# A place of its own for one summed weight block, and other steps for its transfers, for a weight split and for earlier sums

## The chip, the cores and the metric

The kernel runs on one core of a Trainium2 chip. The metric is the time of one execution on the device in microseconds (us); for several runs it is their median.

## The reference, cut to what matters

```python
xn = layernorm(x)                       # x: 1 x 2048 x 576
q, k, v = split(xn @ wqkv)              # 32 heads of 18
pq, pk = phi(q), phi(k)                 # phi(t) = (t + 1 if t > 0 else exp(t)) + 1e-6
o = (pq @ (pk^T v)) / (pq . sum(pk) + 1e-6)   # per head
s = o @ wo
h = gelu(xn @ w1 + b1)                  # 576 -> 4608
g = silu(h @ w2 + b2)                   # 4608 -> 576
out = x + s * g
```

All arrays are float32.

## The kernel before, in words

Each float32 operand of a product is split into a rounded part (hi, a cast on ScalarE) and what is left (lo, a subtraction, mostly on VectorE); three products of such parts stand for one. Large products go by a Strassen-like scheme with seven block products instead of eight. The blocks that it needs besides the plain ones are sums or differences of blocks, made ahead.

The kernel has two parts. The first (up to about 290 us) makes the normalised x, the keys and values and their state, then, in rounds `r` of 14 steps, the queries and the attention output. The second is the feed-forward network. It works in two halves of 1024 rows; each half has nine chunks (`NC`) of 512 of the 4608 hidden columns. A chunk has two `Up` products (x times w1, seven block products each, then gelu), followed by seven block products with w2, numbered in the order 1, 2, 7, 4, 5, 3, 6, each in two parts (`product`, line 1279 for the matmul). A product of a pair 2 after 1, 4 after 7, 3 after 5 goes on in the bank of the earlier one, after VectorE has added that one's result to `macc` (lines 1287 and 1289).

The order is written by hand. A chunk has 28 steps (`NS`): 0 to 13 are the block products of the two Ups, 14 to 27 the halves of the seven products. `add(base + k, f, ...)` puts a call at step k, and `at_step` makes the calls of a step, in the order in which they were added, after that step's matmuls have been issued. TensorE, VectorE, ScalarE and GpSimd (POOL) keep the written order in this part; each engine works through its own instructions one after another, and an instruction that must wait holds up those behind it. SyncE (SP) issues the plain transfers, in its own order.

What the chunk's steps do, as far as the change and its neighbours go:

- `HOps.S(i, pr)`: POOL makes the sums of h for the pair `pr` (lines 1237 to 1246), i = 7, 5, 6, 3; for pair 0 at steps 7, 8, 10, 11, for pair 1 at 13, 14, 15, 15. `hi` (line 912) and `lo` (line 915) split them.
- `W1.T(i)`: POOL makes the differences of w1's blocks (lines 937 to 945), i = 5, 6, 7, 4; 7 and 4 overwrite the loaded block. A chunk does this twice: at steps 0 to 2 for its own second Up (table `P1`), and at steps 24 and 25 for the next chunk's first (table `P0`). Difference 4 overwrites a part of what the block "a" is split from.
- `W2`: the w2 operands of the next chunk. `load_raw` loads four blocks into one buffer (`w2raw`), which the chunk's own operands 1, 7 and 3 still read at steps 3, 4 and 6. Operand 7 is block (0, 1) plus block (1, 1), operand 4 is block (0, 0) plus (1, 0) plus operand 7. These sums are made by transfers that POOL issues and that add to what they find in place (`add_to`, line 497). Before the change, operand 7 is summed in `w2raw` itself, operand 4 in a tile of its own, `w2t4`, that is loaded right after the raw blocks.
- In the rounds of the queries, `w2_load` loads raw w2 blocks, `w2_sum` makes sums in the same accumulating way, and `w2_hi` and `w2_lo` split and store them (lines 506 and 511) for use in the second half and the first chunk.

Steps of the changed transfers in a chunk, before: raw load at 8 (10 in chunk 0); the sum of operand 7 and the first of operand 4, one right after the other, at 16 (17); operand 2's split and then operand 4's second sum at 21 (22); operand 4's split at 27.

Of the kernel before, what the change touches and what calls it, by code (L numbers as in the profile page):

```python
# [8 lines left out]
F32 = mybir.dt.float32  # L9
# [6 lines left out]
P = 128  # L16
S = 2048
D = 576
HD = 288
# [7 lines left out]
CF = 4  # L27
NC = NF // CF
# [14 lines left out]
def linear_attention_gated_ffn(ctx, tc, x, wqkv, wo, w1, b1, w2, b2, out):  # L43
    nc = tc.nc
# [96 lines left out]
    class Weight:  # L141

        def __init__(self, pool, name):
            self.h, self.l = (pool.tile([P, 7, 2, HD], F32R, name=f"{name}_{v}") for v in "hl")
            self.rh, self.rl = (pool.tile([P, D], F32R, name=f"{name}_r{v}") for v in "hl")
# [328 lines left out]
    def w2_blocks(c):  # L474
        return w2[c].rearrange("p (r n a d) -> p r n a d", r=2, n=2, a=2)
# [41 lines left out]
    def add(step, fn, *args):  # L517
        plans.setdefault(step, []).append((fn, args))
# [195 lines left out]
    for p in range(1, NPAIR):  # L714
        plan_pair(p)
        base = p * NSP
# [23 lines left out]
    def q_tiles(r):  # L740
        return [r_bufs[(2 * r + s) % 4] for s in range(2)]
# [11 lines left out]
    base = NPAIR * NSP  # L753
# [237 lines left out]
    for r in range(NPAIR + 2):  # L991
        base = (NPAIR + r) * NSP
# [3 lines left out]
        if r < NPAIR:  # L996
            a, b = q_tiles(r)
# [15 lines left out]
        if 1 <= r < NPAIR:  # L1013
            a, b = q_tiles(r)
# [10 lines left out]
        if 2 <= r <= 6:  # L1025
            add(base, w2_load, r + 2, *((w1p, "wa") if r % 2 == 0 else (w2rp, "w2raw")))
        if r == 2:
            add(base + 8, w2_sum, 2 * r + 5)
        if 3 <= r <= 7:
            n = 2 * r + 3  # L1030
            add(base + 1, w2_sum, n + 1)
            if r < 7:
                add(base + 8, w2_sum, n + 2)
            for j in range(2):
                add(base + 7 + j, w2_hi, n + j)
                add(base + 9 + j, w2_lo, n + j)
        if r == 0:
            phi_exp(a, e_bufs[0]), phi_exp(b, e_bufs[1])
            fold_wo({
# [74 lines left out]
    fr = ctx.enter_context(tc.tile_pool(name="fr", bufs=1, side="right", reuse_waits="tile"))  # L1114
# [67 lines left out]
    class W2:  # L1182


        def __init__(self, n):
            self.n, self.ops, self.tiles = n, {}, {}

        def load_raw(self):
            self.raw = raw = load_w2_raw(self.n) if self.n else w2_raw0[0]
            self.B = lambda r, n: raw[:, r, n]  # L1190
            self.src = {1: self.B(0, 0), 2: self.B(1, 0), 3: self.B(1, 1), 7: self.B(0, 1)}
            if 0 < self.n < NC:
                self.src[4] = fr.tile([P, CF // 2, HD], F32, tag="w2t4", name=f"w2t4_{self.n}", bufs=1)
                nc.sync.dma_start(self.src[4], w2_blocks(self.n)[:, 0, 0])

        def sum7(self):
            add_to(self.src[7], w2_blocks(self.n)[:, 1, 1])
# [235 lines left out]
    def plan_w1(add, w, base, T, hi, lo):  # L1433
        for table, what in ((T, w.T), (hi, w.hi), (lo, w.lo)):
            for i, at in table.items():
                add(base + at, what, i)
# [3 lines left out]
        hi={"a": 0, 6: 1, 7: 2, 5: 3, "b": 4, 4: 4},  # L1440
        lo={"a": 0, 6: 1, 7: 2, 5: 3, "b": 4, 4: 4},
    )
    P0 = dict(
        T={5: 24, 6: 24, 7: 25, 4: 25},
        hi={"a": 14, 6: 25, 7: 26, 5: 26, "b": 27, 4: 27},
        lo={"a": 14, 6: 25, 7: 26, 5: 26, "b": 27, 4: 27},
    )


# [7 lines left out]
        hi={  # L1457
            (1, 0): 7, (2, 0): 9, (7, 0): 10, (1, 1): 11, (2, 1): 12, (7, 1): 15, (4, 0): 16,
            (4, 1): 17, (5, 1): 18, (5, 0): 19, (6, 0): 20, (3, 0): 21, (3, 1): 22, (6, 1): 23,
        },  # L1460
        lo={
            (1, 0): 9, (2, 0): 10, (7, 0): 11, (1, 1): 12, (2, 1): 13, (7, 1): 15, (4, 0): 16,
            (4, 1): 17, (5, 1): 18, (5, 0): 19, (6, 0): 20, (3, 0): 21, (3, 1): 22, (6, 1): 23,
        },
# [4 lines left out]
    w2t = {}  # L1469
# [5 lines left out]
    for step in range(n_chunks):  # L1475
        half, c = divmod(step, NC)
        base = step * NS
        plain = step == n_chunks - 1
        h = HOps(c)
        if half == 0:  # L1480
            plan_w1(add, w1t[2 * step + 1], base, **P1)
            w2c = w2t[step]
            if not step:
                add(base + 2, w2c.sum7)
            for i, at in (PW2 if step else PW2_FIRST).items():
                add(base + at, w2c.hi, i)
                add(base + at, w2c.lo, i)
            if step == 0:
                for i, at in W2_SUMS_FIRST.items():
                    add(at, w2t[0].load, i)  # L1490
        if half == 0 and c < NC - 1:
            add(base + 0, make, W1, w1t, 2 * step + 2)
            add(base + 4, make, W1, w1t, 2 * step + 3)
            add(base + 13, lambda n=2 * step + 2: plan_w1(add, w1t[n], base, **P0))
            make(W2, w2t, step + 1)
            nxt = w2t[step + 1]
            add(base + (8 if step else 10), nxt.load_raw)
            add(base + (16 if step else 17), nxt.sum7)
            add(base + (16 if step else 17), nxt.sum4, 0)
            add(base + 21, nxt.hi, 2)  # L1500
            add(base + 21, nxt.lo, 2)
            add(base + (21 if step else 22), nxt.sum4, 1)
            add(base + 27, nxt.hi, 4)
            add(base + 27, nxt.lo, 4)
            for i, at in W2_SUMS_NEXT.items():
                add(base + at, lambda i=i, n=step + 1: w2t[n].load(i))
        elif not plain:
            add(base + (14 if half == 0 else 7), make, W1Loaded, w1t, 2 * step + 2)
            swap = half == 0
            add(base + (22 if swap else 14), make, W1Loaded, w1t, 2 * step + 3)  # L1510
            if step + 2 < n_chunks:
                make(W2, w2t, step + 1)
                for i, at in W2_NEXT.items():
                    add(base + at + 11 * swap, lambda i=i, n=step + 1: w2t[n].load(i))
            else:
                make(W2, w2t, step + 1)
                add(base + 7, w2t[step + 1].load_raw)
        if not plain:
            if half == 0 and c == NC - 1:
                for k, at in ((2, 12), (3, 12), (1, 13), (0, 13)):  # L1520
                    add(base + at, x_swap, k)
                add(base + 25, silu_first, C11)
                for k in range(2):
                    add(base + 26 + k, combine, C12, nc.vector, slice(2 * k, 2 * k + 2))
                    add(base + 26 + k, combine, C21, nc.gpsimd, slice(2 * k, 2 * k + 2))
            for what in ("S", "hi", "lo"):
                for (i, pr), at in PH[what].items():
                    add(base + at, getattr(h, what), i, pr)
        else:
            for f in range(CF):  # L1530
                w2t[step].plain(f)
                add(base + (1, 2, 3, 8)[f], w2t[step].hi, ("p", f))
                add(base + (2, 3, 8, 9)[f], w2t[step].lo, ("p", f))
        if half == 1 and c == 0:
            add(base, silu_first, C12)
            add(base, silu_first, C21)
            add(base, combine, C22, nc.vector, slice(0, 2))
            add(base + 1, combine, C22, nc.vector, slice(2, 4))
            add(base + 1, silu_first, C22)
        if half == 1 and 1 <= c <= 8:  # L1540
            for k in range(2):
                tiles = {}
                def load(k=k, t=7 + c, tiles=tiles):
                    tiles[0] = finish_tiles(k)
                    finish_load(t, k, tiles[0])
                add(base, load)
                add(base + 4, lambda k=k, t=7 + c, tiles=tiles: finish(t, k, tiles[0]))
        if plain:
            for m in (C12, C21, C22):
                add(base + 4, combine, m, nc.gpsimd)  # L1550
            for t, at in enumerate((5, 5, 7, 13, 5, 12, 12, 12)):
                add(base + at, load_xs, t)
            for b, f, at, lo in (
                (0, 0, 7, 8), (0, 1, 8, 9), (1, 0, 10, 10), (1, 1, 10, 11), (0, 2, 11, 12),
                (0, 3, 12, 13), (1, 3, 13, 13), (1, 2, 13, 13),
            ):
                add(base + at, tail_split, b, f)
                add(base + lo, tail_lo, b, f)
        for j in range(CF // 2):
            n = 2 * step + j  # L1560
            u = Up(n, w1t.pop(n), xs)
            for k, i in enumerate(UP):
                u.step(i)
                h.add(j, u.g)
                at_step(base + 7 * j + k)
        if plain:
            break
        held = {}
        for k, i in enumerate(ORDER):
            for q2 in (0, 2):  # L1570
                product(c, i, q2, [h.ops[i, 0], h.ops[i, 1]], w2t[step].ops[i], held)
                at_step(base + 14 + 2 * k + q2 // 2)
# [36 lines left out]
```

## Time and profile before

| | |
|---|---|
| median of 3 runs | 1119.4 us (1118.47 to 1122.9) |
| the profiled execution | 1122.14 us |
| its span, first to last instruction | 1120.4 us |
| TensorE busy | 1098.9 us, 98% |
| VectorE busy | 810.8 us, 72% |
| ScalarE busy | 505.4 us, 45% |
| POOL busy | 459.5 us, 41% |
| TensorE's mean granted clock | 0.996 |
| moved by DMA | 272.50 MB, mean 243 GB/s |

In the profile's rows an instruction is named by its engine, line and operation, then `output<-inputs` by the program's tile names, and partitions x elements of each. PE is TensorE's matmul, PEld its weight load, DVE VectorE, ACT ScalarE, and SPq a transfer issued by SP. In a row in order of time the first number is the start and the second the duration, in us; the square brackets hold the idle time of the engine before it and what ended that. In a row of a stretch, the first number is its length, then come busy time and (x) number of instructions for PE, PEld, DVE, ACT and POOL, then the granted clock, the busy share of the 16 DMA engines and GB/s.

### The profile page before, as it was taken

What the parts mean: (1) busy time and instruction counts of PE and PEld (TensorE: products, weight loads), DVE (VectorE), ACT (ScalarE), POOL (GpSimd) and SP (SyncE); (2) the same over time, 40 slices, a digit from 0 to 9 for tenths busy, and PEclk for the clock granted to TensorE, in tenths of its full rate; (3) what the DMA queues carried; (4) which work ended last, traced back from release to release, by engine and by line L of the source; (5) the groups of instructions that cost most, each with busy time, mean ns of one, the idle gap of its engine ahead of it and who ended that gap; (6) DMA issues with size and microseconds to landing.
All of it is one profiled execution on the core that took longest, in us unless ns stands there. A gap on an engine that the chain in (4) does not pass through costs nothing.

```text
span 1120.4 us, 18755 instructions
## 1 busy us (share of the span) xinstructions
PE 1098.9 (98%) x6924; PEld 1017.2 (91%) x6924; DVE 810.8 (72%) x1242; ACT 505.4 (45%) x913; POOL 459.5 (41%) x419
## 2 busy tenths in 40 slices
PE   8999999999999999999999999999999999999997
PEld 7899998999898998988989889899898998988987
DVE  6877666656598888988889888666475574664756
ACT  6766554535545454454544544524233242242352
POOL 5854433344354444544545434324224132242340
PEclk9999999999999999999999999999999999999999
DMA  5887747895998679687796879977666666766243
GB/s 202 299 265 275 257 129 216 275 293 197 349 313 336 198 267 316 190 333 225 246 320 180 318 208 373 369 263 261 216 200 225 206 203 210 230 198 223 87 135 120
DMA packets 95818, 272.50 MB, mean 243 GB/s; under 512 B 10413, under 2 KB 21165, under 8 KB 93679
## 3 DMA queue, kind: packets, MB, share of 16 engines
q1 hardware_dynamic: 89391, 258.32, 65.2%
q0 software_dynamic: 6336, 12.98, 7.4%
q8 instruction: 55, 0.90, 0.3%
q14 instruction: 36, 0.29, 0.1%
HBM read 165.05 MB, written 100.01 MB: 237 GB/s over the span
## 4 chain that ended last, share of the span: by engine, by line
PE 90%; DVE 4%; ACT 3%; DMA 1%; issue 1%; POOL 1%; DVEq 0%; POOLq 0%; ACTq 0%
PE pm L1279 32%; PE e L1141 12%; PE a L1141 10%; PE zy L1141 10%; PE ps_s L885 5%; PE pl L411 5%; PE b L1141 4%; PE e L356 2%; PE z L356 2%; PE a L356 2%; PE pd L1402 2%; DVE h_l L915 1%; PE ps_kva L464 1%; DMA kr<-kw 1%; PE b L356 1%
## 5 line engine op out<-in xcount | busy, mean ns | idle before, releaser
L912 ACT CAST h_h<-g 128x512 fp32r<-128x512 f32 x204 | 120.1, 621 | 140.6 <-PE pm L1279 139.5
L915 DVE TENSOR_TENSOR h_l<-g,h_h 128x512 fp32r<-128x512 f32 x204 | 169.3, 830 | 0.0
L1287 DVE TENSOR_TENSOR macc<-macc,pm 128x576 f32<-128x576 f32 x128 | 96.1, 751 | 36.8 <-PE pm L1279 36.7
L1246 POOL TENSOR_TENSOR mid<-g 128x512 f32<-128x512 f32 x34 | 44.0, 1294 | 184.7 <-ACT g L1149 184.7
L1141 PE MATMUL a<-xH,wa 128*128 128x512 f32 x360 | 117.1, 390 | 0.0
L1289 DVE TENSOR_TENSOR macc<-pm,macc 128x576 f32<-128x576 f32 x90 | 68.0, 755 | 18.4 <-PE pm L1279 17.6
L1149 ACT ACTIVATE g<-b,b1c 128x512 f32<-128x512 f32 x36 | 24.8, 688 | 124.5 <-DVE b L1167 124.5
L1141 PEld LDWEIGHTS a<-xH,wa 128*128 128x128 f32 x360 | 67.6, 188 | 13.7
L1141 PE MATMUL e<-xSH,wb 128*128 128x512 f32 x216 | 66.6, 390 | 0.2 <-DVE b L1167 0.2
L1240 POOL TENSOR_TENSOR g<-g 128x512 f32<-128x512 f32 x34 | 49.5, 1456 | 22.3 <-DVE h_l L915 20.9
L1158 ACT COPY mid<-a 128x512 f32<-128x512 f32 x36 | 21.2, 588 | 83.0 <-PE a L1141 82.6
L1141 PE MATMUL a<-xL,wa 128*128 128x512 f32 x144 | 56.2, 391 | 0.0
L1373 POOL TENSOR_TENSOR fin1l<-fin1h,fin1l 128x288 f32<-128x288 f32 x8 | 6.4, 806 | 120.0 <-DMA fin1l<-s_dram 61.6
L1243 POOL TENSOR_TENSOR g<-g 128x512 f32<-128x512 f32 x34 | 49.9, 1467 | 13.1 <-DVE h_l L915 11.8
L1237 POOL TENSOR_TENSOR g<-g 128x512 f32<-128x512 f32 x34 | 50.9, 1496 | 2.7
L1161 DVE TENSOR_TENSOR mid<-b,mid 128x512 f32<-128x512 f32 x36 | 24.7, 685 | 37.5 <-PE b L1141 37.4
L1141 PE MATMUL b<-xSH,w 128*128 128x512 f32 x144 | 50.2, 389 | 0.0
L1141 PE MATMUL zy<-xSH,w 128*128 128x512 f32 x144 | 50.2, 389 | 0.0
L1141 PE MATMUL e<-xSH,w 128*128 128x512 f32 x144 | 50.2, 389 | 0.0
L1141 PE MATMUL zy<-xH,w 128*128 128x512 f32 x144 | 50.2, 389 | 0.0
L1141 PEld LDWEIGHTS e<-xSH,wb 128*128 128x128 f32 x216 | 40.5, 188 | 9.1 <-DVE b L1167 0.6
L915 DVE TENSOR_TENSOR h_l<-mid,h_h 128x512 fp32r<-128x512 f32 x34 | 42.4, 1248 | 6.6 <-ACT h_h L912 6.6
(930 smaller groups left out, 3570.1 us busy)
## 6 DMA issues: line engine op xcount, KB each, us to landing
op<-w SPq DMA_DIRECT2D x72, 256.0 KB
w<-op SPq DMA_DIRECT2D x72, 256.0 KB
w1raw<-w SPq DMA_DIRECT2D x18, 640.0 KB
w2raw<-w SPq DMA_DIRECT2D x10, 1152.0 KB
op_a<-wa SPq DMA_DIRECT2D x18, 640.0 KB
wa<-op_a SPq DMA_DIRECT2D x18, 640.0 KB
op<-w2o SPq DMA_DIRECT2D x19, 576.0 KB
w2r<-w SPq DMA_DIRECT2D x6, 1152.0 KB
```

The lines of the kernel that those rows point to most:

```text
L356: nc.tensor.matmul(ps, st, mv, start=first and n == 0, stop=n == len(seq) - 1, skip_group_check=True,)
L411: nc.tensor.matmul(self.ps[n], st, self.wk(hl, k, n), start=(i == 0), stop=(i == n_all - 1))
L885: nc.tensor.matmul(self.ps[h], st[:, k, :], w[:, k, h * HD : (h + 1) * HD], start=(i == 0), stop=(i == len(self.seq) - 1),)
L912: nc.scalar.copy(pair[0], src)
L915: eng.tensor_tensor(pair[1], src, pair[0].bitcast(F32), op=SUB)
L1141: nc.tensor.matmul(ps.rearrange("p (c j) -> p c j", c=4), st, mv, start=first and n == 0, stop=n == len(seq) - 1, skip_group_check=True,)
L1237: tt(src[5, pr], A(1, 1), A(1, 0), op=SUB)
L1240: tt(src[6, pr], src[5, pr], A(0, 0), op=ADD)
L1243: tt(src[3, pr], src[6, pr], A(0, 1), op=SUB)
L1279: nc.tensor.matmul(ps[:, q, :HD], hs[p][st][:, cs], m[:, p, :], start=(n == 0 and i not in CHAIN), stop=(n == len(seq) - 1), skip_group_ch ...
L1287: nc.vector.tensor_tensor(dst, dst, src, op=SUB)
L1289: nc.vector.tensor_tensor(dst, src, dst, op=ADD)
```

## The change

In the first half's chunks operand 7 gets a tile of its own, `w2t6`, and operand 4 takes `w2t5` instead of `w2t4` (both names are used again only at the very end). Each tile is loaded by a call of its own, `load_sum`: operand 4's at step 0 with its first sum at step 4, operand 7's at step 6 with its sum at step 12. Operand 4's second sum, which adds operand 7, moves to step 20. The raw load stays at its step, and its block (0, 1) is no longer read from chunk 1 on. In table `P0` the split of w1's block "a" (cast, subtraction and store) moves from step 14 to step 24. In the queries' rounds the sum of a chunk's first block moves from step 8 to 5 of the round, and the split of the second block by one step (the cast from 8 to 9, the subtraction and store from 10 to 11).

```diff
         if r == 2:
-            add(base + 8, w2_sum, 2 * r + 5)
+            add(base + 5, w2_sum, 2 * r + 5)
         if 3 <= r <= 7:
             n = 2 * r + 3
             add(base + 1, w2_sum, n + 1)
             if r < 7:
-                add(base + 8, w2_sum, n + 2)
+                add(base + 5, w2_sum, n + 2)
             for j in range(2):
-                add(base + 7 + j, w2_hi, n + j)
-                add(base + 9 + j, w2_lo, n + j)
+                add(base + (7, 9)[j], w2_hi, n + j)
+                add(base + (9, 11)[j], w2_lo, n + j)
...
         def load_raw(self):
             self.raw = raw = load_w2_raw(self.n) if self.n else w2_raw0[0]
             self.B = lambda r, n: raw[:, r, n]
-            self.src = {1: self.B(0, 0), 2: self.B(1, 0), 3: self.B(1, 1), 7: self.B(0, 1)}
-            if 0 < self.n < NC:
-                self.src[4] = fr.tile([P, CF // 2, HD], F32, tag="w2t4", name=f"w2t4_{self.n}", bufs=1)
-                nc.sync.dma_start(self.src[4], w2_blocks(self.n)[:, 0, 0])
+            self.src |= {1: self.B(0, 0), 2: self.B(1, 0), 3: self.B(1, 1)}
+
+        def load_sum(self, i):
+            n = self.n
+            self.src[i] = fr.tile([P, 2, HD], F32, tag=f"w2t{5 + i // 7}", name=f"w2s{i}_{n}", bufs=1)
+            nc.sync.dma_start(self.src[i], w2_blocks(n)[:, 0, i // 7])
...
     P0 = dict(
         T={5: 24, 6: 24, 7: 25, 4: 25},
-        hi={"a": 14, 6: 25, 7: 26, 5: 26, "b": 27, 4: 27},
-        lo={"a": 14, 6: 25, 7: 26, 5: 26, "b": 27, 4: 27},
+        hi={"a": 24, 6: 25, 7: 26, 5: 26, "b": 27, 4: 27},
+        lo={"a": 24, 6: 25, 7: 26, 5: 26, "b": 27, 4: 27},
     )
...
             if not step:
+                w2c.src[7] = w2c.B(0, 1)
                 add(base + 2, w2c.sum7)
...
             nxt = w2t[step + 1]
+            add(base + 0, nxt.load_sum, 4)
+            add(base + 4, nxt.sum4, 0)
+            add(base + 6, nxt.load_sum, 7)
+            add(base + 12, nxt.sum7)
             add(base + (8 if step else 10), nxt.load_raw)
-            add(base + (16 if step else 17), nxt.sum7)
-            add(base + (16 if step else 17), nxt.sum4, 0)
             add(base + 21, nxt.hi, 2)
             add(base + 21, nxt.lo, 2)
-            add(base + (21 if step else 22), nxt.sum4, 1)
+            add(base + 20, nxt.sum4, 1)
             add(base + 27, nxt.hi, 4)
             add(base + 27, nxt.lo, 4)
```

More of the change, by code (lines that the diff above doesn't have):

```diff
@@ L1185, in __init__ @@
         def __init__(self, n):
-            self.n, self.ops, self.tiles = n, {}, {}
+            self.n, self.ops, self.tiles, self.src = n, {}, {}, {}
         def load_raw(self):
```

## The prediction

> **What bounds the kernel now.** I read the page first (busy shares), then the chain that ended last, then the instructions of one steady chunk of the first half in order of time, then the DMA share of stretches of it.
>
> ```profile
> span 1120.4 us, 18755 instructions
> PE 1098.9 (98%) x6924; PEld 1017.2 (91%) x6924; DVE 810.8 (72%) x1242; ACT 505.4 (45%) x913; POOL 459.5 (41%) x419
> ```
>
> TensorE bounds the span, so a change is worth only the TensorE stalls that it removes or makes. The chain lists the fourth product of every chunk at equal places, so that their distances are the chunks' lengths:
>
> ```profile
> 295.39 1.81 PE e L1141 x8
> ...
> 314.00 22.41 PE pm L1279 x168
> ...
> 340.55 1.81 PE e L1141 x8
> ...
> 663.58 1.81 PE e L1141 x8
> ...
> 708.68 1.81 PE e L1141 x8
> ```
>
> Chunk 0 takes 45.16 us, the last chunk of the first half (663.58 to 708.68), which the change leaves out, 45.10. The seven between (340.55 to 663.58) take 323.03, or 46.15 each: 1.05 us too long, 7.35 in all. Only chunks 0 to 7 of the first half are changed, so 7.35 us is about all that can be won there. The chain inside one of the seven (it starts its down products at 451.26) shows where the 1.05 lies, and the engines' rows show why:
>
> ```profile
> 451.26 12.88 PE pm L1279 x96
> ...
> 466.86 1.91 DVE h_l L915
> ...
> 468.81 6.00 PE pm L1279 x43
> ```
>
> ```profile
> 466.56 0.87 POOL L497 DMA_DIRECT2D w2t<-w2raw  x1 [5.48 <-DMA w2t<-w]
> ...
> 466.78 1.98 DVE L915 TENSOR_TENSOR h_l<-g,h_h 128x512 fp32r<-128x512 f32 x1
> ...
> 467.12 1.07 POOL L937 TENSOR_TENSOR w1t<-w1raw 128x256 f32<-128x256 f32 x1
> ```
>
> POOL waits 5.48 us for the accumulating transfers before it issues operand 4's second sum; w1's differences, which stand behind it, then run beside a VectorE subtraction, which takes 1.98 us. Product 3 waits for that subtraction.
>
> **The change part by part.** *Second sum of operand 4 at step 20, after a product-7 sum of step 12.* POOL's 5.48 us wait goes, w1's differences run some 6 us earlier, and the late subtraction is short again. Price: the 1.05 us, seven times: -7.35.
>
> *w1's first block split at step 24 instead of 14.* One cast, one subtraction and one store of 640 KB move.
>
> ```profile
> 453.57 1.21 DVE L915 TENSOR_TENSOR wa<-w1raw,wa 128x640 fp32r<-128x640 f32 x1
> ...
> 471.65 0.75 DVE L1287 TENSOR_TENSOR macc<-macc,pm 128x576 f32<-128x576 f32 x1 [0.39 <-PE pm L1279]
> ...
> 473.25 0.75 DVE L1287 TENSOR_TENSOR macc<-macc,pm 128x576 f32<-128x576 f32 x1 [0.51 <-PE pm L1279]
> ```
>
> VectorE has 0.39 + 0.51 us idle at steps 25 and 26, near the 1.21 us it must take in; TensorE is not ahead of it there, and the block is wanted only at the next chunk's first product. Nothing, with up to 0.3 us a chunk if VectorE stays late. POOL's last difference must now wait for that subtraction; POOL has nothing behind it in the chunk. SP's store (0.66 MB, 1.8 us of the engines at 372 GB/s, a rate shown below) comes to lie just ahead of the stretch in which the DMA engines are full; if a quarter of it falls inside, 0.4 us of delay there, else none.
>
> *First load and sum of operand 4 at steps 0 and 4.* One more SP issue ahead of the w1 stores, and a wait on POOL ahead of the sum of h for product 7, pair 0 (POOL's next work):
>
> ```profile
> 433.78 0.80 SPq L923 DMA_DIRECT2D w1raw<-w  x1
> ...
> 441.61 1.29 POOL L1246 TENSOR_TENSOR mid<-g 128x512 f32<-128x512 f32 x1 [8.08 <-ACT g L1149]
> ```
>
> The load would be issued at about 434.6, and 7 us pass until POOL is wanted. Even 2 us late, POOL's chain of four has its idle time behind it to absorb that: nothing.
>
> *Product 7's own load at step 6 and its sum at step 12.* This is the disputed term. The load is issued where now the raw block's is, at about 444.3; POOL comes to the sum right after its fourth sum, at 448.94 (447.64 + 1.30), and behind the sum stands the first of pair 1's four sums.
>
> ```profile
> 444.34 0.45 SPq L767 DMA_DIRECT2D w2raw<-w  x1
> ...
> 447.64 1.30 POOL L1243 TENSOR_TENSOR g<-g 128x512 f32<-128x512 f32 x1 [0.70 <-DVE h_l L915]
> ...
> 452.81 1.29 POOL L1246 TENSOR_TENSOR mid<-g 128x512 f32<-128x512 f32 x1 [3.86 <-ACT g L1149]
> ...
> 454.13 0.62 ACT L912 CAST h_h<-mid 128x512 fp32r<-128x512 f32 x1 [0.79 <-POOL mid L1246]
> ...
> 455.37 1.12 DVE L915 TENSOR_TENSOR h_l<-mid,h_h 128x512 fp32r<-128x512 f32 x1
> ...
> 459.29 0.88 POOL L497 DMA_DIRECT2D w2raw<-w  x1
> ...
> 459.81 0.74 DVE L1287 TENSOR_TENSOR macc<-macc,pm 128x576 f32<-128x576 f32 x1
> ...
> 460.70 0.50 PE L1279 MATMUL pm<-w__5066,h_h 128*128 128x288 f32 x2
> ```
>
> When does that load land? Stretches, with DMA share and GB/s at the end of each row:
>
> ```profile
> 429.00:453.00 24.00, 24.00 (x114) 20.15 (x113) 19.66 (x29) 13.40 (x25) 9.05 (x9) 1.00 0.99 372
> 453.00:455.00 2.00, 2.00 (x17) 2.00 (x17) 2.00 (x3) 1.21 (x3) 1.92 (x2) 1.00 0.11 40
> ...
> 460.80:465.60 4.80, 4.80 (x38) 4.80 (x38) 4.41 (x8) 2.41 (x5) 0.28 (x1) 1.00 0.84 123
> 465.60:466.40 0.80, 0.80 (x8) 0.80 (x8) 0.80 (x2) 0.00 (x0) 0.00 (x0) 1.00 0.00 0
> 309.00:322.00 13.00, 13.00 (x84) 12.10 (x84) 12.09 (x16) 7.30 (x12) 9.12 (x6) 1.00 1.02 416
> ```
>
> From 429 to 453 the DMA engines are full. The last two transfers of that backlog, the raw block and operand 4's quarter of one (128 x 2304 and 128 x 576 floats, 1.18 + 0.29 MB), take 4.0 us at 372 GB/s, so all ahead of them is through at about 449.0. To that come, ahead of or with the new load's end: its own quarter block (0.8 us), operand 4's earlier load (0.8) and operand 4's first accumulating sum. Two such sums alone kept the engines at 0.84 for 4.80 us, or 2.0 each. Together 452.6; the slowest engines ran about 1 us past the mean (0.11 still after 453), so I take 453.6. After the two sums' data ended (share 0.00 from 465.60) POOL began at 466.56: 1.0 us more. The issue holds POOL 0.56 (466.56 to 467.12). Pair 1's first sum then starts at X = 455.2 instead of 452.81.
>
> The raw block, now behind it on SP, is read first at step 21 (451.26 + 7 x 1.6 us, a fourteenth of 22.41 each, 462.5) and lands by about 457: nothing.
>
> What X costs: the subtraction of product 7's h can start at X + 2.0 (1.32 to the cast, 0.62 for it). From its start now, 455.37, to product 4's start, 460.70, 5.33 us pass with VectorE full (the accumulation at 459.81 must read the bank that product 4 adds to). So product 4 starts at X + 7.33; undelayed it would at about 460.58. The stall is X - 453.25, so 1.95 us in place of 1.05. Bounds: if the accumulating sum takes nothing from the queue and no engine lags, the load lands at 450.6 and POOL is free at 452.2: no stall. If the lag is 2 us and the moved store adds 0.4, X = 456.6: 3.35. I take 1.95, since each of its parts has a row here: +13.65 for seven chunks.
>
> Chunk 0 has no stall now, but its queue is longer:
>
> ```profile
> 307.53 0.32 SPq L909 DMA_DIRECT2D op<-w__3710  x1
> ...
> 309.26 0.33 SPq L1217 DMA_DIRECT2D w__3743<-op  x1
> 310.69 0.33 SPq L767 DMA_DIRECT2D w2raw<-w  x1
> ...
> 323.31 0.89 POOL L497 DMA_DIRECT2D w2raw<-w  x1 [1.23 <-DMA w2raw<-w]
> ```
>
> The raw block ended near 322.3 (323.31 less 1.0). It and the three transfers of 0.59 MB between it and the new load's place (307.53 to 309.26) are 2.95 MB, 7.1 us at 416 GB/s: 315.2. With 0.7 + 0.7 + 2.0 the new load lands at 318.6 and X is 320.2. Down products start at 314.00 here, so the bound is 316.0 (453.25 - 451.26 + 314.00): +4.2, between 0 and 5.
>
> *Queries.* POOL's sum at step 5 instead of 8, one cast and one subtraction a step later:
>
> ```profile
> 225.22 0.88 POOL L497 DMA_DIRECT2D w2r<-w  x1 [7.11 <-DMA w2r<-w]
> ...
> 239.30 0.68 ACT L506 CAST w2o<-w2r 128x576 fp32r<-128x576 f32 x1
> ...
> 242.34 0.87 PE L853 MATMUL ptp<-ident,pbuf 128*128 128x128 f32 x3 [2.35 <-DVE th L865]
> ```
>
> These sums already wait for a landing, with POOL idle, so an earlier place starts none earlier. The cast at 239.30 stands ahead of the copies that the one large stall waits for; moved behind them it may give back its 0.6: -0.6, else 0.
>
> Sum: -7.35 + 13.65 + 4.2 - 0.6 = +9.9 us on the profiled span of 1120.4 (that execution took 1122.1, the median of the runs is 1119.4). Taken to the median: 1129.3, or 1129.
>
> The Trainium skill ("DMA: Bandwidth & Descriptors", Anatomy of one DMA) gives a transfer about 2.0 us plus its bytes at 436 GB/s. By that the new load would land 2.7 us after issue, at 447.0, ahead of POOL, and the sum would be -8.0. The rows of chunk 0 disagree: the raw block issued at 310.69 released POOL at 323.31, 12.6 us later, where that sentence would have 4.7 (an estimate from the page).
>
> **The rivals.** *The loads land in time* (the opposite side). If the new load has landed by 451.7, POOL is free by 453.25, and no stall is left: -7.35 - 0.6, 1111.4. For it: the wait on POOL now is real and goes. Against: the full DMA share to 453. *Partly in time.* If the accumulating sum is served late and takes nothing from the queue, with the 1 us lag: landing 451.6, X 453.2, chunk 0 about +2: -7.35 + 2 - 0.6, 1113.4; with half of the sum's time taken X is 454.2, or 0.95 a chunk, and chunk 0 +3.2: 1121.3. *A second stall.* w1's differences now run beside the subtractions for product 5, each then some 0.4 us longer (1.12 beside POOL at 455.37). Product 3 may then find the bank that it adds to not yet read; at most that 0.4 a chunk: +2.8, 1132. *The wait stays* (the change doesn't do what it says): product 7's sum, issued at 454.6, needs some 6 us to land while POOL's four sums end at X + 6.5 = 461.7; it may hold POOL a little, and then the second stall is the same as now, 1.05 seven times: 1137.
>
> **How the numbers follow.** Late load with a longer stall, second stall and kept wait included: 0.58. Partly in time, about as before: 0.22. In time: 0.20. The likeliest alone spans 1124 (X 0.6 earlier, chunk 0 +3) to 1140 (the upper bound of X, chunk 0 +5); with both signs the range is 1112 to 1138. A difference of 0.5% (5.6 us) is about what can be told from none. Slower by more 0.57, within 0.23, faster by more 0.20.
>
> **What would show it.** Right: POOL idle 4 to 7 us before product 7's sum, released by its load's DMA; pair 1's first sum some 2 to 4 us later against the down products; the stall now before product 7 or 4, at 20 us and not 28 us into the chunk; no 5 us wait before the second sum of operand 4. The chunks would be 47 us, chunk 0 49. Wrong: chunks of 45.1 us, or POOL's idle before product 7's sum under 4.3 us.

## The result and the profile after

| | before | after |
|---|---|---|
| median of 6 runs each | 1120.7 us (1118.5 to 1122.9) | 1132.9 us (1129.3 to 1135.1) |
| ratio to before, 95% interval | | 1.0108 [1.0086, 1.0129] |
| the profiled execution | 1122.14 us | 1134.17 us |

The changed kernel is 12 us slower. First come two rows of its page, the span and the busy times, in the form of those shown of before.

```profile
span 1132.5 us, 18755 instructions
...
PE 1099.5 (97%) x6924; PEld 1014.4 (90%) x6924; DVE 809.5 (71%) x1242; ACT 502.6 (44%) x913; POOL 458.1 (40%) x419
```

TensorE works as long as before (1099.5 against 1098.9 us) in a span that is 12.1 us longer: nearly all of the loss is idle time of TensorE. The chain that ended last, again by the fourth product of the chunks (start, duration, piece):

```profile
293.15 1.83 PE e L1141 x8
...
342.29 1.81 PE e L1141 x8
...
390.52 1.81 PE e L1141 x8
...
439.52 1.81 PE e L1141 x8
...
485.88 1.81 PE e L1141 x8
...
675.21 1.81 PE e L1141 x8
...
720.31 1.81 PE e L1141 x8
```

The eight changed chunks run from 293.15 to 675.21, 382.06 us, where before they took 368.19: 13.87 more. Chunk 0 takes 49.1, chunks 1 to 7 47.6 on average (332.92 / 7) and unevenly: 48.2, 49.0 and 46.4 for 1 to 3. The untouched chunk after them takes 45.10, as before. Ahead of chunk 0, where the queries' steps changed, 2.24 us were won (293.15 against 295.39); the rest of the program differs by 0.5.

The view of waits says what POOL stands for at the accumulating transfers (total, times, longest); the first row is of the kernel before.

```profile
POOL w2t L497 <- DMA w2t<-w: 43.1, 8, 5.6
```

After:

```profile
POOL w2s L497 <- DMA w2s<-w: 97.4, 16, 10.4
```

In place of eight waits of 5.4 us stand sixteen of 6.1, at nearly every sum into an operand's own block (one more, of 9.1 us in chunk 0, is put down to TensorE; see further down). POOL works through its list in order, so what counts is what stands behind them. Chunk 2 after, instructions in order of time from SP's issue of product 7's load:

```profile
401.71 0.90 POOL L497 DMA_DIRECT2D w2s<-w  x1 [10.33 <-DMA w2s<-w]
...
402.79 1.04 SPq L1196 DMA_DIRECT2D w2s<-w  x1
...
408.96 0.42 PE L1281 MATMUL pm<-w__4651,h_h 128*128 128x288 f32 x2
...
413.77 0.90 POOL L497 DMA_DIRECT2D w2s<-w  x1 [4.72 <-DMA w2s<-w]
...
414.38 1.61 POOL L1248 TENSOR_TENSOR mid<-g 128x512 f32<-128x512 f32 x1
...
416.03 0.62 ACT L912 CAST h_h<-mid 128x512 fp32r<-128x512 f32 x1 [5.11 <-POOL mid L1248]
...
416.68 1.21 DVE L915 TENSOR_TENSOR h_l<-mid,h_h 128x512 fp32r<-128x512 f32 x1 [3.44 <-ACT h_h L912]
...
417.95 0.40 PE L1281 MATMUL pm<-w__4676,h_l 128*128 128x288 f32 x1 [0.72 <-DVE h_l L915]
...
420.69 0.90 POOL L497 DMA_DIRECT2D w2s<-w2s  x1
...
422.12 0.50 PE L1281 MATMUL pm<-w__4568,h_h 128*128 128x288 f32 x2 [1.36 <-DVE macc L1289]
```

The load that SP issues at 402.79 releases POOL at 413.77, 11 us later. Until then pair 1's first sum of h (L1248) stands behind the accumulating transfer, and from it the delay goes straight down the rows: sum, cast, subtraction, product 7, and product 4 at 422.12. The old wait is gone (420.69 has none). The DMA engines were as busy as before while the load lay in the queue; a stretch of the same profile:

```profile
389.00:409.00 20.00, 20.00 (x90) 16.53 (x89) 16.53 (x23) 10.41 (x21) 8.27 (x7) 1.00 1.00 358
```

### The profile page after: what moved, and what is told of

It reads as the page before. It is cut to its first block, busy times and chain, and to the rows that moved or that the text cites. A ratio compares the mean times of both kernels' runs of the same rounds, so it can differ in the third digit from the quotient of the medians.

```text
span 1132.5 us, 18755 instructions
## 1 busy us (share of the span) xinstructions
PE 1099.5 (97%) x6924; PEld 1014.4 (90%) x6924; DVE 809.5 (71%) x1242; ACT 502.6 (44%) x913; POOL 458.1 (40%) x419
## 4 chain that ended last, share of the span: by engine, by line
PE 78%; DMA 9%; DVE 4%; ACT 3%; issue 3%; POOL 2%; SPq 1%; DVEq 0%; POOLq 0%; ACTq 0%
PE pm L1281 30%; PE e L1141 9%; PE a L1141 8%; PE zy L1141 8%; PE pl L411 5%; DMA w2s<-w 4%; PE b L1141 4%; PE ps_s L885 3%; DMA op<-w 2%; PE e L356 2%; PE pd L1404 2%; PE z L356 2%; PE a L356 2%; PE ps_kva L464 1%; DMA kr<-kw 1%
## 5 line engine op out<-in xcount | busy, mean ns | idle before, releaser
L915 DVE TENSOR_TENSOR h_l<-g,h_h 128x512 fp32r<-128x512 f32 x204 | 172.7, 847 | 0.0
L1248 POOL TENSOR_TENSOR mid<-g 128x512 f32<-128x512 f32 x34 | 48.9, 1438 | 91.6 <-ACT g L1149 91.6
L1242 POOL TENSOR_TENSOR g<-g 128x512 f32<-128x512 f32 x34 | 50.9, 1497 | 17.1 <-DVE h_l L915 15.4
L497 POOL DMA_DIRECT2D w2s<-w x16 | 14.2, 889 | 104.8 <-DMA w2s<-w 95.7
L1245 POOL TENSOR_TENSOR g<-g 128x512 f32<-128x512 f32 x34 | 52.3, 1537 | 10.7 <-DVE h_l L915 9.0
L915 DVE TENSOR_TENSOR h_l<-mid,h_h 128x512 fp32r<-128x512 f32 x34 | 39.4, 1159 | 21.8 <-ACT h_h L912 21.8
```

Source lines behind the costliest of these rows:

```text
L915: eng.tensor_tensor(pair[1], src, pair[0].bitcast(F32), op=SUB)
L1242: tt(src[6, pr], src[5, pr], A(0, 0), op=ADD)
L1245: tt(src[3, pr], src[6, pr], A(0, 1), op=SUB)
L1248: tt(src[7, pr], A(0, 0), A(1, 0), op=SUB)
```

## The experiments

My theory was the prediction's: product 7's sum holds POOL ahead of pair 1's sums until its late load has landed. Its rivals were the split of "a" at step 24, a VectorE that is too full, and the other moved steps. The first four runs part the change into the queries, the old stall, the landing and the order on POOL; three more take single steps, and the last is a version that avoids the wait. X stands below for the start of pair 1's first sum, counted from the chunk's first down product.

### The queries' steps alone

Before, with only this:

```diff
-            add(base + 8, w2_sum, 2 * r + 5)
+            add(base + 5, w2_sum, 2 * r + 5)
...
-                add(base + 8, w2_sum, n + 2)
+                add(base + 5, w2_sum, n + 2)
...
-                add(base + 7 + j, w2_hi, n + j)
-                add(base + 9 + j, w2_lo, n + j)
+                add(base + (7, 9)[j], w2_hi, n + j)
+                add(base + (9, 11)[j], w2_lo, n + j)
```

> The kernel before with the three edits of the queries' rounds alone. In the two traces the first product of the feed-forward part starts at 291.13 us before and 288.88 after, 2.2 us earlier. Theory (the gain comes from these edits and is kept to the end): 2 us faster than before, 45.1 us for chunk 0, 46.1 for chunks 1 to 7. Rival (the earlier start is lost again because chunk 0 waits for its transfers, which come no earlier): chunk 0 about 1 us longer, the whole within 1 us of before.

Measured: 1116.8 against 1120.0 us, ratio 0.9971 [0.9955, 0.9987]. This part of the change makes the kernel faster, by about 3.3 us. Something else came out as well. The chunks' code is that of before, yet in the profiled execution four of the seven ran without their stall (45.2 us), the others at 45.9 to 46.3. Of the 7.8 us between its span and that of before, 3.4 lie ahead of the first chunk and 4.1 in these seven chunks, so the 3.3 us of the median need not all come from the queries' part. Chunk 4 of this kernel has it, chunk 5 has not; their rows in order of time, chunk 4 first:

```profile
508.14 0.88 POOL L497 DMA_DIRECT2D w2t<-w2raw  x1 [5.53 <-DMA w2t<-w]
508.30 2.04 DVE L915 TENSOR_TENSOR h_l<-g,h_h 128x512 fp32r<-128x512 f32 x1
508.70 1.07 POOL L937 TENSOR_TENSOR w1t<-w1raw 128x256 f32<-128x256 f32 x1
...
554.62 0.68 DVE L915 TENSOR_TENSOR h_l<-g,h_h 128x512 fp32r<-128x512 f32 x1
554.75 0.89 POOL L497 DMA_DIRECT2D w2t<-w2raw  x1 [5.85 <-DMA w2t<-w]
555.22 0.75 DVE L1287 TENSOR_TENSOR macc<-macc,pm 128x576 f32<-128x576 f32 x1
555.31 1.09 POOL L937 TENSOR_TENSOR w1t<-w1raw 128x256 f32<-128x256 f32 x1
```

Where the subtraction of h starts 0.13 us ahead of POOL's release, it is over in 0.68 when w1's difference begins; where it starts 0.16 after, it lies beside the difference and takes 2.04. The old stall hangs on a few tenths of a microsecond.

### The old stall alone: w1's differences ahead of the wait

Before, with one line:

```diff
-        T={5: 24, 6: 24, 7: 25, 4: 25},
+        T={5: 20, 6: 20, 7: 20, 4: 20},
```

> The kernel before with w1's four differences of the next chunk put at step 20, ahead of operand 4's second sum. It tests what made the 1.05 us in each of chunks 1 to 7. Theory (POOL's wait for operand 4's transfers let the differences run beside the subtraction that product 3 waits for): these chunks take 45.1 us, the whole is 7.3 us faster than before, and POOL still waits 2 us or more at operand 4's second sum, with nothing behind it. Rival (VectorE is too full wherever the differences run, and the stall only moves to product 5 or 3): chunks over 45.6 us, under 4 us gained.

Measured: 1121.3 against 1120.0 us, ratio 1.0010 [0.9993, 1.0027]. Its chain that ended last, the fourth products of chunks 2 and 3, and its view of waits:

```profile
389.20 1.81 PE e L1141 x8
...
434.85 1.81 PE e L1141 x8
```

```profile
POOL w2t L497 <- DMA w2t<-w: 9.7, 8, 1.5
```

The numbers are those set for the rival (over 45.6 us a chunk, under 4 us gained), and the theory's 45.1 is missed. POOL's wait shrinks from 5.4 to 1.2 us, as the differences are done ahead of it, and the chunks go from 46.15 to 45.65: half of the stall goes with the wait, the other half stays. That VectorE is too full wherever the differences run would explain it, but no run shows it. The gain of 3.5 us over seven chunks is not to be seen in the time: in the profiled execution chunk 0 lost 1.1 of it, and a stall in the queries' part, shown further down, 1.9.

### The landing: product 7's load earlier

The changed kernel, with the load asked for at step 0 and two buffers for it; the sum stays at step 12:

```diff
-            self.src[i] = fr.tile([P, 2, HD], F32, tag=f"w2t{5 + i // 7}", name=f"w2s{i}_{n}", bufs=1)
+            self.src[i] = fr.tile([P, 2, HD], F32, tag=f"w2t{5 + i // 7 * 2}", name=f"w2s{i}_{n}", bufs=1 + i // 7)
...
+            add(base + 0, nxt.load_sum, 7)
...
-            add(base + 6, nxt.load_sum, 7)
```

> The changed kernel with product 7's own load at step 0, right behind operand 4's, in two buffers (with one it would wait for the chunk's own split of operand 7). Its sum stays at step 12. Theory (pair 1's sums of h wait behind the sum of product 7 for the landing of its load): the load lands some 8 us before step 12, POOL does not wait there, pair 1's first sum starts 1.7 us after the down products begin as before the change, and chunks 1 to 7 take 45.1 to 45.4 us; the whole 1113 to 1117. Rival (VectorE's longer queue, from the differences that run earlier and the split of w1's first block at step 24): the stall of 1.2 to 3.9 us a chunk stays, 1128 or more.

Measured: 1114.2 against 1120.0 us, ratio 0.9947 [0.9930, 0.9965]. POOL around the same place, chunk 3, in order of time:

```profile
440.64 0.88 POOL L497 DMA_DIRECT2D w2s<-w  x1 [8.49 <-DMA w2s<-w]
...
449.15 0.90 POOL L497 DMA_DIRECT2D w2s<-w  x1
451.61 1.28 POOL L1248 TENSOR_TENSOR mid<-g 128x512 f32<-128x512 f32 x1 [1.56 <-ACT g L1149]
```

Product 7's sum (449.15) no longer waits, and pair 1's first sum waits for its own operand, gelu's result, instead of a transfer. Chunks 1 to 7 fall to 45.1 to 45.7, chunk 0 to 47.3. Operand 4's first sum still waits 8.5 us, mostly without harm (the Ups of chunk 0 take 1.1 us longer than before, those of the others 0.3 at most).

The load went out far earlier than the edit's six steps. SP keeps its own order, and with the second buffer it issued each of these loads a chunk ahead: three of the sixteen own loads fall in chunk 0 and only one in chunk 7. The load for the sum at 449.15 in chunk 3 is this one, in chunk 2:

```profile
399.06 1.12 SPq L1196 DMA_DIRECT2D w2s<-w  x1
```

So the run shows that the stall is gone when the load has landed in time; it does not show how much earlier would have been enough.

### The order: product 7's sum behind pair 1's sums

The changed kernel, with the load left where it is:

```diff
-        T={5: 24, 6: 24, 7: 25, 4: 25},
+        T={5: 20, 6: 20, 7: 20, 4: 25},
...
-            add(base + 12, nxt.sum7)
+            add(base + 16, nxt.sum7)
...
-            add(base + 20, nxt.sum4, 1)
+            add(base + 21, nxt.sum4, 1)
```

> The changed kernel with product 7's sum at step 16, behind pair 1's four sums on POOL, operand 4's second sum at 21 and w1's differences 5, 6 and 7 at 20. All loads stay where the change has them, so the DMA queue is as full as in the changed kernel up to step 12. Theory (what costs is only that POOL, in its order, stands in front of pair 1's sums): their first starts 1.7 us after the down products begin, chunks 1 to 7 take 45.1 to 45.4 us, the whole 1113 to 1117. Rival (the fuller DMA queue or VectorE's order costs, wherever POOL waits): chunks over 46 us, the whole 1125 or more.

Measured: 1114.9 against 1120.0 us, ratio 0.9948 [0.9934, 0.9963]. Its view of waits, and POOL in order of time:

```profile
POOL w2s L497 <- DMA w2s<-w: 86.5, 16, 10.6
```

```profile
449.66 1.29 POOL L1248 TENSOR_TENSOR mid<-g 128x512 f32<-128x512 f32 x1 [2.80 <-ACT g L1149]
...
455.67 0.90 POOL L497 DMA_DIRECT2D w2s<-w  x1
```

POOL still waits 86.5 us in all, nearly as long as in the changed kernel (97.4), now at operand 4's two sums. Chunks 1 to 7 take 45.1 to 45.6, chunk 0 46.0. It is not the wait that costs, but the wait ahead of pair 1's sums. Load early and sum late each take the loss away: the cause is the meeting of the two.

### The split of "a" back at step 14

```diff
-        hi={"a": 24, 6: 25, 7: 26, 5: 26, "b": 27, 4: 27},
-        lo={"a": 24, 6: 25, 7: 26, 5: 26, "b": 27, 4: 27},
+        hi={"a": 14, 6: 25, 7: 26, 5: 26, "b": 27, 4: 27},
+        lo={"a": 14, 6: 25, 7: 26, 5: 26, "b": 27, 4: 27},
```

> The changed kernel with the split of w1's first block back at step 14. Theory (the landing of product 7's load sets the stall, VectorE only waits): pair 1's first sum still starts 2.7 to 5.4 us after the down products begin, chunks 1 to 7 stay 1.2 to 3.9 us too long, the whole within 4 us of the changed kernel (1129 to 1137). Rival (the 1.2 us of VectorE work at step 24 makes part of the stall, such as the 0.2 us before product 3): chunks 0.2 us or more shorter each, or longer if VectorE at step 14 is full.

Measured in two runs: 1129.4 against 1121.1 us, ratio 1.0091 [1.0064, 1.0117]; chunks 1 to 7 take 46.9 to 47.9, with X from 2.8 to 4.4. The stall stays, so the split is not its cause. It may be a small part of it, as the rival has it: these chunks are 0.3 us shorter on average than in the changed kernel (47.26 against 47.56), and X is 3.5 instead of 4.0. With one profile of each, and chunks that differ by more, that is not shown; the intervals of the two kernels' ratios overlap.

### Operand 4's first sum behind product 7's

The changed kernel, with the first accumulating transfer out of the queue while the load of product 7 lies in it:

```diff
-        T={5: 24, 6: 24, 7: 25, 4: 25},
+        T={5: 20, 6: 20, 7: 20, 4: 25},
...
-            add(base + 4, nxt.sum4, 0)
+            add(base + 16, nxt.sum4, 0)
...
-            add(base + 20, nxt.sum4, 1)
+            add(base + 21, nxt.sum4, 1)
```

> The changed kernel with operand 4's first accumulating sum at step 16 instead of 4, so that its transfer is not in the DMA queue while product 7's load waits there; its second sum at 21 and w1's differences 5, 6 and 7 at 20, so that POOL's wait for it has nothing behind it. The prediction gave that sum 2.0 us of the queue. Theory: product 7's load lands about 2 us earlier against the chunk's start, pair 1's first sum starts 1.7 to 3.4 us after the down products begin (2.7 to 5.4 in the changed kernel), and the whole is 8 to 15 us faster than the changed kernel. Rival (the sum takes nothing from the queue): pair 1's first sum as late as in the changed kernel, the whole within 5 us of it.

Measured: 1122.2 against 1121.1 us, ratio 1.0022 [1.0005, 1.0039]. Chunk 3's POOL in order of time (down products begin at 450.87):

```profile
453.40 0.89 POOL L497 DMA_DIRECT2D w2s<-w  x1 [4.68 <-DMA w2s<-w]
454.01 1.60 POOL L1248 TENSOR_TENSOR mid<-g 128x512 f32<-128x512 f32 x1
```

X falls from a mean of 3.97 to 2.5 in chunks 1 to 7, and these chunks to 45.3 to 46.7, as the theory has it. Of the 1.5 us, 1.1 lie between SP's issue of the load and POOL's release (8.85 us on average, 9.9 in the changed kernel), and 0.4 come from an earlier issue. So the accumulating sum costs the load behind it 1.1 to 1.5 us on average (I had priced it at 2.0), and of the 2.46 us that chunks 1 to 7 lost, 1.0 stays without it. The edit also moves w1's differences and the second sum, as the run with product 7's sum at step 16 did; in POOL's order these stand behind pair 1's first sum. Chunk 0's Ups take 22.7 us again, where the changed kernel took 24.1: the sum at step 4 was to blame there too.

### The later cast alone

Before, with only the split of the second w2 block moved (the two `(7, 9)[j]` and `(9, 11)[j]` lines of the first experiment); the sums stay at step 8.

> The kernel before with the queries' split of the second block one step later (cast 9, subtraction and store 11), the sums left at step 8. In the run with all three edits the stall near 240 us was 1.4 us instead of 2.6 and the granted clock stayed at 1.00 after it instead of 0.71. Theory (the cast stood in front of the copies for which the transposition waits): the same as with all three edits, 3 us faster than before, with the clock at 1.00 after the stall. Rival (the earlier sums do it): as before, a stall of 2.4 us or more and a lower clock after it, within 1 us of before.

Measured: 1117.0 against 1121.1 us, ratio 0.9972 [0.9954, 0.9989], the same as all of the queries' edit. The sums at step 5 add nothing that shows. ScalarE before, in order of time, and then in this kernel:

```profile
239.30 0.68 ACT L506 CAST w2o<-w2r 128x576 fp32r<-128x576 f32 x1
...
240.46 0.71 ACT L860 CAST th<-ptp 128x640 fp32r<-128x640 f32 x1
```

```profile
239.04 0.69 ACT L860 CAST th<-ptp 128x640 fp32r<-128x640 f32 x1
...
240.31 0.67 ACT L506 CAST w2o<-w2r 128x576 fp32r<-128x576 f32 x1
```

The weight cast no longer stands ahead of `th`, on which TensorE waits. And the clock: a stretch of 4 us behind that stall, before (and below it the part at the lower clock), in the second experiment's kernel (which has the queries as before) and in this one (last columns: clock, DMA share, GB/s).

```profile
243.00:247.00 4.00, 4.00 (x24) 4.00 (x24) 2.45 (x4) 1.00 (x2) 1.20 (x2) 0.71 0.97 324
...
241.93:245.33 3.40, 2.99 (x13) 3.02 (x14) 2.64 (x3) 0.71 (x3) 2.27 (x2) 0.50 0.98 329
```

```profile
243.00:247.00 4.00, 4.00 (x18) 4.00 (x19) 2.18 (x2) 0.99 (x3) 1.77 (x2) 0.50 1.01 349
```

```profile
243.00:247.00 4.00, 4.00 (x32) 4.00 (x32) 3.72 (x10) 0.99 (x2) 0.49 (x2) 1.00 1.00 248
```

With the cast ahead, TensorE stands for 2.35 us (the row at 242.34 in the prediction), and the clock is 0.50 for 3.41 us from 241.92; 0.71 is the mean of the 4 us shown, in which 24 matmuls start. In the second experiment's kernel TensorE stood 4.18 us, and the clock was 0.50 for 6.83 us. With the cast later it stands for 1.78 us, the clock keeps 1.00, and 32 matmuls start. In all eight kernels with the later cast the stall there is at most 1.78 us and the clock behind it 1.00. Over the runs, the mean granted clock of this kernel is 0.999 (10 runs), of before 0.997 (19). So in the queries' part the gain is the shorter stall, 0.6 us, and the clock behind it.

That is not the whole difference. Of the 5.3 us between the spans of the two profiled executions, 2.6 lie ahead of the first chunk and 2.8 in chunks 1 to 7, of which three (3, 5 and 7) ran without the old stall, with the code of before. Whether the queries' edit causes that, and how the 3 us of the median divide, stays open.

### Loads a chunk ahead

The changed kernel, with each chunk loading both blocks for the chunk after the next, asked for in its down products (two buffers), and the sums in the place that is then free:

```diff
-            add(base + 0, nxt.load_sum, 4)
-            add(base + 4, nxt.sum4, 0)
-            add(base + 6, nxt.load_sum, 7)
-            add(base + 12, nxt.sum7)
+            add(base + (4 if step else 16), nxt.sum7)
+            add(base + (4 if step else 16), nxt.sum4, 0)
+            if step < NC - 2:
+                make(W2, w2t, step + 2)
+                for i in (7, 4):
+                    add(base + 16, w2t[step + 2].load_sum, i)
...
-            add(base + 20, nxt.sum4, 1)
+            add(base + 21, nxt.sum4, 1)
```

Also w1's differences are at `T={5: 20, 6: 20, 7: 20, 4: 25}`, the tiles have `bufs=2`, and chunk 0 loads those of chunk 1 at its steps 0 and 6.

> A version meant to beat both: the changed kernel with the two own loads issued a chunk earlier at step 16, where the DMA engines are little used, in two buffers each, both first sums at step 4, operand 4's second sum at 21, w1's differences 5, 6 and 7 at 20; chunk 0 loads as the change does and sums at 16. Theory (only landings that POOL waits for in front of other work cost): no wait of POOL before pair 0's or pair 1's sums from chunk 1 on, chunks 0 to 7 45.1 to 45.3 us, 1108 to 1112 in all. Rival (two accumulating sums at step 4, in the full DMA stretch, delay other loads or pair 0's sums): chunks over 45.5 us, 1114 or more.

Measured: 1111.7 against 1121.1 us, ratio 0.9933 [0.9915, 0.9952], faster than both kernels. Its POOL in order of time, and the chain that ended last:

```profile
429.56 1.79 POOL L497 DMA_DIRECT2D w2s<-w  x2
...
448.89 1.29 POOL L1248 TENSOR_TENSOR mid<-g 128x512 f32<-128x512 f32 x1 [3.85 <-ACT g L1149]
```

```profile
402.25 22.39 PE pm L1281 x168
...
447.35 22.39 PE pm L1281 x168
```

From chunk 1 on both first sums go out without a wait. The loads were issued 2 to 6 us ahead of the down products, where the DMA engines are full (share 1.04 from 440 to 447 us) and not little used; what the loads have is time, some 30 us until the sums. The down products run through without a gap (168 matmuls in 22.39 us), 45.10 us from one chunk to the next, with 45.24 in chunk 0.

## Why the prediction came out right, point by point

**The time.** Predicted was +9.9 us on the profiled execution; it was +12.1, and 1132.9 us as a median lies in the range. The 2.2 between are +3.6 in chunks 1 to 7, -0.2 in chunk 0, -1.6 in the queries and +0.5 elsewhere (rounded). The sign came from the step it was said to come from, as the load-early and the sum-late run show from two sides.

**The landing and X.** Predicted: X = 4.1 us, counted from the first down product as in the measurements (455.2 less 451.10; the chain's piece at 451.26 begins a little later). Measured in chunks 1 to 7: 2.7 to 5.4, mean 3.97. From SP's issue to POOL's release 10.3 us were reckoned (444.3 to 454.6); measured were 8.2 to 11.0, on average 9.9. So the sum over the backlog (what is queued at the measured rate, the accumulating sum, 1 us of lag, 1 us to POOL) held on average. That it held to 0.1 us in X is partly luck: the accumulating sum, in it at 2.0, was worth 1.1 to 1.5 when it was taken out, and the spread of 2.7 us between chunks was not foreseen.

**From X to the stall.** Predicted: product 4 starts at X + 7.33, and a chunk takes 1.95 more than 45.10. Measured: X + 7.7 to 7.8 in every chunk (in chunk 2, 422.12 - 414.38 = 7.74), mostly because POOL's sum took 1.6 there and not 1.29. Chunks 1 to 7 took 2.46 too long on average. The term is too small by 0.5 a chunk, 3.6 in all: 0.4 by this longer way, and 0.25 by a stall ahead of product 3, the "second stall" of the rivals, less 0.1 for the earlier X.

**The split of "a" at step 24.** Predicted: nothing, 0.3 us a chunk at most. The run with it back at step 14 has chunks 0.3 shorter on average; if that is the split's, it is the upper bound that came.

**Chunk 0.** Predicted +4.2, measured +4.0 (49.12 - 45.13), but by another way, so this is a right number with a wrong step. X was only 3.7 after the first down product and not 6.4 (320.2 less 313.84), and yet the products took 2.6 more. The other 1.4 lie in the second Up, where the step "first load and sum of operand 4: nothing" failed. POOL and VectorE there, after, in order of time, and TensorE's row of the waits:

```profile
303.41 0.86 POOL L497 DMA_DIRECT2D w2s<-w  x1 [9.11 <-PE b L1141]
...
303.82 2.39 DVE L915 TENSOR_TENSOR w__3715<-w2raw,w__3715 128x576 fp32r<-128x576 f32 x1
303.97 1.62 POOL L1248 TENSOR_TENSOR mid<-g 128x512 f32<-128x512 f32 x1
```

```profile
PE e L1141 <- DVE b L1167: 1.1, 1, 1.1
```

POOL waits 9.1 us for operand 4's load, so the sum of h falls beside VectorE's split of operand 7, which takes 2.39; the `b` that TensorE needs comes behind that. The releaser named, a TensorE product, had long been done; it is the transfer that ended last, as the profiles of the kernels with the sum at 16 and the split at 14 name it at this place. In the other chunks the same wait of 8 to 10 us is absorbed, as predicted.

**POOL's idle time ahead of product 7's sum.** Predicted 4 to 7 us, and under 4.3 as a sign of being wrong. It was 2.9 to 4.7, with the stall there all the same: POOL came 1 to 2.3 us later itself, counted from the down products, since the wait before operand 4's sum had held up pair 0's sums. The sign was badly chosen; X is the better one.

**Where the stall is.** Product 7 and product 4, as predicted (417.95 and 422.12 in chunk 2; in chunks 3 to 5 product 4 alone). The "20 and 28 us into the chunk" were miscounted: by the prediction's own rows product 4 stands 28 us after the chunk's fourth product (460.70 less 340.55 + 2 x 46.15) and the old stall 36; measured in chunk 2 were 27 (417.95 - 390.52) and 32.

**The old stall.** Its 1.05 a chunk went, as predicted, and in the runs without the new wait the chunks fall to 45.1 to 45.7. The second experiment shows that taking away POOL's wait alone is worth half of it; all of it went in the kernels that also move the split of "a" to 24. That this split is what gives the other half is argued, not shown, and the run with it back at step 14 does not bear it out: product 3 waits 0.25 us there, as in the changed kernel.

**Queries.** Predicted -0.6, measured -2.2 in the profile and -3.3 as a median when alone. The place was right (the cast ahead of the copies), the term far too small: it priced the cast's 0.6 us, which is what the stall lost (2.35 to 1.78), and left out the clock behind it. The -3.3 may hold a part from chunks that ran without the old stall.

**The rivals.** "The loads land in time" is what the load-early run shows (1114.2; 1111.4 was worked out for it), and the loads a chunk ahead reach 1111.7. "Partly in time" had 1113.4 us if operand 4's first sum takes nothing from the queue; the run with that sum out of the way came to 1122.2, since 1.0 us a chunk stays even so. "The wait stays" did not come: at 420.69 POOL goes on without one.

## What to carry to other kernels

A transfer that waits for data is an instruction in its engine's list like any other: before it is moved, look up what is queued behind it there, and let it stand behind what TensorE needs next. A plain transfer's place in the code says little of when SP issues it: in two of these kernels the loads went out elsewhere than meant, so look it up in the trace. To price its landing, add up the bytes that are already in the DMA queues at the rate the profile shows, and count accumulating transfers as more than their bytes. Where a second buffer lets a load go out a stage earlier, the landing need not be priced at all: that took the chunks to 45.10 us here, where the new place of the sum had made 47.6 of 46.15.

## What the runs showed of the hardware that I had not expected

**A full queue.** With the DMA engines fully busy, a load of 0.29 MB took 11 us from SP's issue to POOL's release in chunk 2, about as long as the 1.18 MB one of chunk 0 before (310.69 to 323.31, 12.6 us). At the measured 358 to 416 GB/s their own data take 0.8 and 3 us, so most of both is the queue ahead.

**The clock after short gaps.** The traces' granted clock is 1.00 or 0.50, and in the queries' part it stays at 0.50 for 3.41 us or twice that. A gap of TensorE of 2.35 us near 240 was followed by 3.41 us at 0.50, one of 4.18 us by 6.83, and gaps of up to 1.78 us there by none. But a stall of 1.53 us at 182, the same in both kernels, lowered it before and not after (stretches of 4 us, before first):

```profile
182.00:186.00 4.00, 2.46 (x12) 2.37 (x12) 3.93 (x8) 0.26 (x1) 0.91 (x2) 0.74 0.94 378
```

```profile
182.00:186.00 4.00, 2.46 (x19) 2.43 (x19) 3.93 (x8) 0.13 (x1) 0.91 (x2) 1.00 0.92 368
```

Of seven traces with this stall two show the lower clock behind it, so a gap of this length is a matter of chance. The Trainium skill ("TensorE: Matmul & The Clock Gate", What's actually happening) has the clock halved after an idle window of about 3.4 us that runs freely, not from the gap's start. The chance and the 3.41 us fit a free window; that gaps of 1.53 and 2.35 us are enough does not fit a window idle for its whole length.

**Subtractions beside POOL.** The subtraction of h takes 0.68 us alone and mostly 1.0 to 2.04 beside POOL's sums, while the accumulation `macc`, which reads one operand from PSUM, stays at 0.75 beside them (555.22 and 555.31 in the first experiment). The Trainium skill ("SBUF — State Buffer", Who interferes with whom) says that a VectorE instruction with two inputs in SBUF contends with POOL's reads and one with a single such input does not; most of these rows agree.
